# LayerNorm scale, shift and Strassen differences on row tiles, halves turned by DMA; low halves of q and of outputs ahead of p's, low products last

## The chip, the cores and the metric

The kernel runs on one core of one Trainium2 chip. The metric is the device time of one execution in microseconds (us). Before the change it is 1780.32 us, the median of three runs between 1778.46 and 1781.55 us. TensorE is called PE in the profile, VectorE DVE, ScalarE ACT, GpSimd POOL; SP is the queue that issues the DMAs.

## What is computed

One transformer block on 2048 rows of 512 values: LayerNorm with scale and shift from a condition vector, attention of 32 heads over the last 512 keys of a cache with 8 key heads, a gated residual, a second LayerNorm with scale and shift, a GEGLU network with 1792 hidden columns, a gated residual.

```
mod = (silu(c) @ w_mod).reshape(c.shape[0], 6, 1, -1)
sa, ca, ga, sb, cb, gb = mod[:, 0], mod[:, 1], mod[:, 2], mod[:, 3], mod[:, 4], mod[:, 5]
h = _layernorm(x) * (1 + ca) + sa
q = h @ wq;  s = q @ k.T * Dh ** -0.5;  p = softmax(s);  x = x + ga * ((p @ v) @ wo)
h = _layernorm(x) * (1 + cb) + sb
x = x + gb * ((gelu(h @ w_gate) * (h @ w_up)) @ w_down)
```

## The kernel before, in words

**Three products for one.** All operands are float32 values that are split in two float16 halves, a high one (ACT, rounding) and a low one (what is left, by DVE or POOL). `mm3` makes one product out of three float16 matmuls of 128x128 by 128x512 into one PSUM bank: low by high (line 86), high by low (line 87), high by high (line 88). The stationary operand comes first in the names, so in the scores the first of the three is the one that needs the low half of q.

**Stages.** The rows are treated in two halves of 1024. Four times, called gen 0 to 3, a normed half is prepared: gen 0 and gen 1 for the attention of half 0 and 1, gen 2 and gen 3 for the network of half 0 and 1. Each half consists of two blocks of 512 rows, and the products of a prepared half with the weights (q, and the network's first layer) are done by Strassen's scheme with seven instead of eight block products. It needs, transposed to columns on partitions and split in halves, the plain blocks b11, b21, b22 and the four differences t1 to t4.

**How gens 1 to 3 are prepared** (`ln_tile`, `combos`). A tile of 128 rows is loaded (in gen 2 it is the accumulator itself), DVE computes mean and variance, POOL the inverse root (line 386), DVE norms it in one instruction (line 466; ACT does it in gen 2, line 465), PE turns it by four float32 transposes into PSUM (line 471), ACT applies scale and shift by column in four instructions (line 479), the result `hf` is stored to DRAM (`hs`). In gens 1 and 2, ACT and POOL also make the halves of the plain blocks from it (lines 491, 493). When all eight tiles are done, `combos` loads the columns again (`cb`), POOL subtracts (line 510), ACT rounds (line 363), POOL makes the low half (line 367).

**The main loop.** Time in the attention runs in slots t = 0 to 511, one for each score tile of 128 rows by 512 keys. In slot t stand PE's scores of t; on DVE their maximum (line 914), the reciprocals of two row sums (line 931), the low half of p of slot t-3 (line 940), and then the things put into the slot's "d" list, among them the low halves of q and of the attention's outputs (line 676); on ACT the row sums' scaling (line 928), the exponential of t (line 923) and the high half of p of t-2 (line 935). Then SP issues a DMA transpose that turns p (line 944), and PE takes other products from a list. `run("d")`, `run("x")`, `run(t)` and `run("w")` are the places of a slot at which planned work is put in. Every engine works its list in order; SP too, so that a DMA which has to wait holds back those behind it. p is turned four slots at a time into `pt`, and the product with v (`po`) of unit u = t // 4 is taken two units later.

**Plans.** Loads into the five `raw` buffers are planned by `sched` (a position for the load's first use, from which the load goes ahead by up to three slots when the buffer's last user allows), others are put at a fixed slot by `at`, or between two slots by `within`. `mod_load` brings the weights from which DVE computes the scale and shift columns of the second LayerNorm (`wmc`, line 135), from slot 239 on.

Of the kernel before, what the change touches and what calls it, by code (L numbers as in the profile page):

```python
# [14 lines left out]
ALU = mybir.AluOpType  # L15
# [48 lines left out]
def block_kernel(ctx: ExitStack, tc: tile.TileContext, x, kT, v, wq, wo, wg, wu, wd, cT, wc, wm, out):  # L64
# [20 lines left out]
    def mm3(ps, lhi, llo, rhi, rlo, first, last, chain=False):  # L85
        nc.tensor.matmul(ps, llo, rhi, start=first, stop=False, skip_group_check=chain)  # L86
        nc.tensor.matmul(ps, lhi, rlo, start=False, stop=False, skip_group_check=chain)  # L87
        nc.tensor.matmul(ps, lhi, rhi, start=False, stop=last, skip_group_check=chain)  # L88
# [254 lines left out]
    NB = 14  # L343
    BK, hs, y1 = {}, {}, {}

    def spilled(gen, key):
        if (gen, key) not in hs:
            n = KT if key in (0, 1) else 2
            hs[gen, key] = dram.tile([P, n, QB], F32, name=f"hs{gen}_{key}")
        return hs[gen, key]  # L350

    def block(gen, name):
        if (gen, name) not in BK:
            BK[gen, name] = pool.tile([P, 4, QB], F16, tag="h", name=name, bufs=NB)
        return BK[gen, name]

    def stored(gen, name, p):
        qb, dt = {"b11": (0, p), "b21": (0, 2 + p), "y": (1, p), "b22": (1, 2 + p)}.get(name, (None, None))
        return spilled(gen, name)[:, p, :] if qb is None else spilled(gen, qb)[:, dt, :]

    def put(gen, name, p, src, eng):
        def high():
            nc.scalar.activation(block(gen, name)[:, p, :], src(), AF.Copy)

        def low():
            t = block(gen, name)
            eng.tensor_tensor(t[:, 2 + p, :], src(), t[:, p, :], op=ALU.subtract)

        return high, low

    def ln_cols(key):
        return (1, 0) if key == "a" else (4, 3)
# [40 lines left out]
    def ln_out(qb, dt):  # L413
# [11 lines left out]
        def affine(act=True):  # L425
            st["f"] = pool.tile([P, D], F32, tag="ot", name="hf", bufs=NOT) if qb else tmp("hf")
            if act:
                nc.scalar.activation(st["f"], st["ps"], AF.Identity, scale=cols[:, 1, dt:dt + 1], bias=cols[:, 0, dt:dt + 1])
            else:
                ts(st["f"], st["ps"], cols[:, 1, dt:dt + 1], cols[:, 0, dt:dt + 1], op1=ALU.add)  # L430
            dma(spilled(0, qb)[:, dt, :], st["f"])

        def direct():
            nc.scalar.activation(block(0, name)[:, p, :], st["ps"], AF.Identity, scale=cols[:, 1, dt:dt + 1], bias=cols[:, 0, dt:dt + 1])

        def low(eng=nc.vector):
            t = block(0, name)
            eng.tensor_tensor(t[:, 2 + p, :], st["f"], t[:, p, :], op=ALU.subtract)
# [5 lines left out]
    def ln_tile(gen, i, src):  # L444
        jsc, jsh = ln_cols("a" if gen < 2 else "f")
        qb, i = divmod(i % (2 * QT), QT)
        st = {}

        def load():
            if gen == 2:  # L450
                st["x"] = src()
            else:
                st["x"] = raw("xs")
                dma(st["x"], src())

        def stat():
            ln_stat(st["x"], st)
            ln_power(st)
            if gen == 2:
                st["nm"] = small.tile([P, 1], F32, name="nmean")  # L460
                pool_ts(st["nm"], st["mv"][:, 0:1], st["rs"], -1.0)

        def norm():
            if gen == 2:
                return nc.scalar.activation(st["x"], st["x"], AF.Identity, bias=st["nm"], scale=st["rs"])
            nc.vector.tensor_scalar(st["x"], st["x"], st["mv"][:, 0:1], st["rs"], op0=ALU.subtract, op1=ALU.mult)

        def turn():
            st["ps"] = bank("acc", "pln", NACC)
            for dt in range(KT):  # L470
                nc.tensor.transpose(st["ps"][:, dt * P:(dt + 1) * P], st["x"][:, dt * P:(dt + 1) * P], ident)

        def affine(dts):
            if 0 in dts:
                st["f"] = raw("hf") if gen == 2 else tmp("hf")
            f = st["f"]
            for dt in dts:
                sl = slice(dt * P, (dt + 1) * P)
                nc.scalar.activation(f[:, sl], st["ps"][:, sl], AF.Identity,
                                     scale=cols[:, jsc, dt:dt + 1], bias=cols[:, jsh, dt:dt + 1])  # L480
            if KT - 1 in dts:
                dma(spilled(gen, qb)[:, :, i * P:(i + 1) * P], f.rearrange("p (k q) -> p k q", k=KT))

        def parts(act):
            o = slice(i * P, (i + 1) * P)
            f = st["f"].rearrange("p (k q) -> p k q", k=KT)
            for h, name in enumerate(("b11", "b21") if qb == 0 else (None, "b22")):
                if name:
                    t, src = block(gen, name), f[:, 2 * h:2 * h + 2, :]
                    if act:  # L490
                        nc.scalar.activation(t[:, 0:2, o], src, AF.Copy)
                    else:
                        nc.gpsimd.tensor_tensor(t[:, 2:4, o], src, t[:, 0:2, o], op=ALU.subtract)

        more = [lambda: parts(True), lambda: parts(False)] if gen < 3 else []
        return load, [stat, norm, turn, lambda: affine((0, 1)), lambda: affine((2, 3))] + more

    def combos(gen, p, eng, base=True, d=0, e=0):
        X = {}

        def load(name):
            if gen == 0 and (p == 0 or name in ("b21", "b22")):
# [4 lines left out]
            dma(X[name], stored(gen, name, p))  # L507
# [4 lines left out]
        def parts(pos, name, tile_):  # L512
            high, low = put(gen, name, p, lambda: X[tile_], eng)
            return [(pos, high), (pos + 1 + e, low)]

        def plain(pos, name):
            return parts(pos, name, name) if base else []

        return [
            (lambda: load("b11"), plain(0, "b11") + [(2, diff("b11", "y", "b11"))] + parts(d + 4, "t1", "b11")),  # L520
            (lambda: load("y"), [(2, nop), (3, diff("y", "b22", "y"))] + parts(d + 5, "t3", "y")),
            (lambda: load("b22"), (plain(1, "b22") or [(2, nop)]) + [(4, diff("b22", "b22", "b11"))] + parts(d + 6, "t2", "b22")),
            (lambda: load("b21"), plain(3, "b21") + [(5, diff("b21", "b21", "b22"))] + parts(d + 7, "t4", "b21")),
# [262 lines left out]
    def product(key, gen, k, bank_of, start, stop):  # L786
        a, b = PROD[k]

        def group(p):
            c, off = COL[a]  # L790
            w, m = SET[key][c], BK[gen, b]
            sl = slice(off + p * P, off + (p + 1) * P)
            mm3(bank_of(), w[:, 0, sl], w[:, 1, sl], m[:, p, :], m[:, 2 + p, :], start and p == 0, stop and p == 1, True)
# [51 lines left out]
    def q_plain(u):  # L845
# [4 lines left out]
        def group(kt):  # L850
            if kt == 0:
                st["p"] = bank("acc", "pq", NACC)
            w, m, p = SET[u // 4][h % 2], BK[0, names[kt // 2]], kt % 2
            sl = slice(kt * P, (kt + 1) * P)
            mm3(st["p"], w[:, 0, sl], w[:, 1, sl], m[:, p, :], m[:, 2 + p, :], kt == 0, kt == KT - 1)
# [34 lines left out]
    def attn_final(ti):  # L890
# [3 lines left out]
        if ti < 2 * QT:  # L894
            own, steps = ln_tile(2, ti, lambda: acc[ti])
            own()
            for d, fn in zip((1, 4, 5, 6, 7, 9, 10), steps):
                at(("w", now[0] + d), fn)
            at(now[0] + 9, lambda: load_acc(nxt, rows_of(x, nxt)))
        else:  # L900
            at(now[0] + 3, lambda: load_acc(nxt, y1[nxt]))
# [15 lines left out]
    def expo(t):  # L917
# [6 lines left out]
        E[t].update(e=e, sm=sm)  # L924

    def recips(t):
        r = small.tile([P, 2], F32, name="rr", bufs=4)
        nc.scalar.activation(r, E[t]["sm"], AF.Copy, scale=1.0 / PSC)  # L928
        for k in range(2):
            E[t + k]["r"] = r[:, k:k + 1]  # L930
        return lambda: nc.vector.reciprocal(r, r)  # L931
# [55 lines left out]
    def q_first(warm):  # L987
        ps = bank("acc", "pq", NACC)
        for term, (a, b) in enumerate(((0, 0), (1, 0), (0, 2))):
            for kt in range(KT):  # L990
                w, m, p = SET[0][0], BK[0, ("b11", "b21")[kt // 2]], kt % 2
                nc.tensor.matmul(ps, w[:, a, kt * P:(kt + 1) * P], m[:, b + p, :], start=term + kt == 0, stop=term == 2 and kt == KT - 1)
# [4 lines left out]
    def begin():  # L997
# [10 lines left out]
        block(0, "y")  # L1008
        for name in ("b11", "b21", "b22", "t3", "t2", "t4", "t1"):
            block(0, name)  # L1010
# [94 lines left out]
    def sched_combos(gen, p, base):  # L1105
        for k, (load, steps) in enumerate(combos(gen, p, nc.gpsimd if gen or p == 0 else nc.vector, False, 0 if gen else 1 if p else 2, 0 if gen or p else 5)):
            if gen == 0 and (p == 0 or k > 1):
# [6 lines left out]
    for p in range(2):  # L1114
        sched_combos(0, p, CB[p])

    def plan_gen(gen, t_ln, t_cb, dcb, src):
        for i in range(2 * QT):
            t = t_ln[i]
            load, steps = ln_tile(gen, i, lambda i=i: src(i))  # L1120
            sched(t, (load, steps[:3]), t + 3, t + 5)
            for off, fn in zip((6, 7, 8, 9), steps[3:]):
                at(("w", t + off), fn)
        for p in range(2):
            sched_combos(gen, p, t_cb + dcb * p)

# [456 lines left out]
```

## Time and profile before

| | before |
|---|---|
| median of the runs | 1780.32 us (1778.46 to 1781.55) |
| span of the profiled execution, first to last instruction | 1775.9 us |
| its own time by the runs | 2.6 to 5.7 us of each run lie around such a span |
| PE / DVE / ACT / POOL busy | 98% / 81% / 68% / 49% |
| DMA engines, mean busy share | 0.80 over the span |
| chain that ended last, PE's share | 76% |

The profiled execution's own time is given as its span alone; the runs' times also hold what lies ahead of the first and behind the last instruction. A matmul of 512 columns is shown as 379 ns long, but the next one starts 216 ns after it, so that PE's busy share counts overlapped time, and a gap below some 160 ns between two matmuls does not show as idle time. Work is counted by the number of matmuls in a stretch instead.

### The profile page before, as it was taken

To read this page: it belongs to the slowest core of one execution; us is meant where nothing else is said; L and a number is where in the kernel's file an instruction comes from. 1 tells how busy PE (TensorE), PEld (TensorE's weight loads), DVE (VectorE), ACT (ScalarE), POOL (GpSimd) and SP (SyncE) were. 2 spreads that over 40 slices of the span, in tenths; PEclk is the share of its full clock that TensorE was granted. 3 is DMA by queue.
4 is the path that set the end of the run, shared out by engine and by line. 5 is a ranking of instruction groups with operands and counts; after the bars stand their busy time and mean duration, and the time that the engine had idled before them with its cause. 6 is when DMAs were issued, how large, how long until landed. Compare 5 with 4: busy or idle time off the path is not lost.

```text
span 1775.9 us, 25975 instructions
## 1 busy us (share of the span) xinstructions
PE 1732.4 (98%) x8112; PEld 796.0 (45%) x8114; DVE 1445.0 (81%) x2509; ACT 1216.4 (68%) x2822; POOL 877.5 (49%) x1103
## 2 busy tenths in 40 slices
PE   7899999999999989999999999999999999999999
PEld 4444444444444434444444444444444444444443
DVE  7888888888888889888888888888885768766676
ACT  5887787878878767887777777777774455434342
POOL 4879878776788873435565565555420024000000
PEclk9999999999999999999999999999999999999999
DMA  7999999999999997999999999999985543252222
GB/s 229 212 195 212 214 217 200 222 204 220 217 213 230 205 198 165 196 201 231 209 209 207 209 217 205 210 207 215 190 174 134 185 141 123 68 182 80 86 75 74
DMA packets 662122, 327.62 MB, mean 184 GB/s; under 512 B 553056, under 2 KB 575840, under 8 KB 661984
## 3 DMA queue, kind: packets, MB, share of 16 engines
q1 hardware_dynamic: 661696, 325.44, 79.8%
q8 instruction: 64, 1.05, 0.3%
q14 instruction: 74, 0.61, 0.1%
q10 hardware_dynamic: 288, 0.52, 0.1%
HBM read 131.73 MB, written 59.90 MB: 108 GB/s over the span
## 4 chain that ended last, share of the span: by engine, by line
PE 76%; DVE 12%; ACT 6%; issue 2%; DMA 2%; POOL 2%; SPq 0%; DVEq 0%; POOLq 0%; ACTq 0%
PE py L86 7%; PE py L87 7%; PE py L88 7%; PE ps L86 5%; PE ps L88 5%; PE ps L87 5%; PE po L86 4%; PE po L88 4%; PE po L87 4%; DVE p L940 3%; PE fa L86 3%; PE fa L88 2%; PE fa L87 2%; DVE nm L914 2%; PE qa L86 2%
## 5 line engine op out<-in xcount | busy, mean ns | idle before, releaser
L923 ACT ACTIVATE ee<-ps,nm 128x512 f32<-128x512 f32 x512 | 351.2, 686 | 256.4 <-DVE nm L914 250.6
L940 DVE SCALAR_TENSOR_TENSOR p<-ee,rr,p 128x512 f16<-128x512 f32 x512 | 467.1, 912 | 0.2
L914 DVE TENSOR_REDUCE nm<-ps 128x1 f32<-128x512 f32 x512 | 349.1, 682 | 83.5 <-PE ps L88 82.1
L935 ACT ACTIVATE p<-ee,rr 128x512 f16<-128x512 f32 x512 | 365.1, 713 | 0.9 <-DMA pt<-p 0.7
L86 PE MATMUL ps<-k,qt 128*128 128x512 f16 x512 | 194.3, 379 | 19.1 <-DVE qt L676 18.6
L86 PE MATMUL py<-wo,ot 128*128 128x512 f16 x512 | 194.1, 379 | 1.6 <-DVE ot L676 1.6
L88 PE MATMUL ps<-k,qt 128*128 128x512 f16 x512 | 194.2, 379 | 0.0
L87 PE MATMUL ps<-k,qt 128*128 128x512 f16 x512 | 194.2, 379 | 0.0
L87 PE MATMUL po<-pt,v 128*128 128x512 f16 x512 | 194.0, 379 | 0.0
L88 PE MATMUL po<-pt,v 128*128 128x512 f16 x512 | 194.0, 379 | 0.0
L87 PE MATMUL py<-wo,ot 128*128 128x512 f16 x512 | 194.0, 379 | 0.0
L88 PE MATMUL py<-wo,ot 128*128 128x512 f16 x512 | 194.0, 379 | 0.0
L86 PE MATMUL po<-pt,v 128*128 128x512 f16 x512 | 194.0, 379 | 0.0
L931 DVE RECIPROCAL rr<-rr 128x2 f32<-128x2 f32 x256 | 41.3, 161 | 95.8 <-ACT rr L928 94.4
L386 POOL TENSOR_TENSOR rs<-rs,nhalf 128x1 f32<-128x1 f32 x32 | 19.5, 609 | 187.3 <-DVE rs L380 99.1
L86 PEld LDWEIGHTS <-w 128*128 128x128 f16 x728 | 71.3, 98 | 88.7 <-DMA w<-kept 2.9
L87 PEld LDWEIGHTS <-w 128*128 128x128 f16 x728 | 71.3, 98 | 87.7 <-issue 3.2
L88 PEld LDWEIGHTS <-w 128*128 128x128 f16 x728 | 71.3, 98 | 86.3 <-issue 0.7
L884 DVE SCALAR_TENSOR_TENSOR acc<-py,dysc,acc 128x512 f32<-128x512 f32 x112 | 81.6, 746 | 28.8 <-PE py L88 28.0
L884 DVE SCALAR_TENSOR_TENSOR acc<-py,ysc,acc 128x512 f32<-128x512 f32 x128 | 94.6, 739 | 10.9 <-PE py L88 10.9
L923 ACT ACTIVATION_READ_ACCUMULATOR ee<-ps,nm 128x1 f32 x512 | 100.7, 197 | 0.0
L86 PEld LDWEIGHTS <-qt 128*128 128x128 f16 x512 | 50.3, 98 | 81.8 <-DVE qt L676 25.9
(267 smaller groups left out, 3859.6 us busy)
## 6 DMA issues: line engine op xcount, KB each, us to landing
w<-kept SPq DMA_DIRECT2D x123, 256.0 KB, 3.2
wo<-kept SPq DMA_DIRECT2D x60, 256.0 KB, 3.7
raw<-in_wo SPq DMA_DIRECT2D x56, 256.0 KB, 3.2
kept<-stage SPq DMA_DIRECT2D x56, 256.0 KB, 3.3
kept<-w SPq DMA_DIRECT2D x39, 256.0 KB, 3.4
rw<-in_wq SPq DMA_DIRECT2D x38, 256.0 KB, 3.3
hs<-hf SPq DMA_DIRECT2D x32, 256.0 KB, 2.7
pt<-p SPq DMA_TRANSPOSE x512, 3.5
```

Source lines behind the costliest of these rows:

```text
L86: nc.tensor.matmul(ps, llo, rhi, start=first, stop=False, skip_group_check=chain)
L87: nc.tensor.matmul(ps, lhi, rlo, start=False, stop=False, skip_group_check=chain)
L88: nc.tensor.matmul(ps, lhi, rhi, start=False, stop=last, skip_group_check=chain)
L386: nc.gpsimd.tensor_tensor(st["rs"], st["rs"], nhalf, op=ALU.pow)
L884: nc.vector.scalar_tensor_tensor(acc[ti], st["p"], by, acc[ti], op0=ALU.mult, op1=ALU.add)
L914: nc.vector.tensor_reduce(nm, E[t]["ps"], axis=AX.X, op=ALU.max, negate=True)
L923: nc.scalar.activation(e, E[t]["ps"], AF.Exp, bias=E[t]["nm"], scale=1.0, accum_out=sm[:, t % 2:t % 2 + 1])
L931: return lambda: nc.vector.reciprocal(r, r)
L935: nc.scalar.activation(p16[:, 0, :], E[t]["e"], AF.Copy, scale=E[t]["r"])
L940: nc.vector.scalar_tensor_tensor(p16[:, 1, :], E[t]["e"], E[t]["r"], p16[:, 0, :], op0=ALU.mult, op1=ALU.subtract)
```

## The change

Gens 1 to 3 are prepared in another way (`ln_pair`, with `plan_pair` for the slots). Two tiles, of the same place in the two blocks of 512 rows, go together. DVE applies mean, scale, inverse root and shift in two instructions on row tiles, with the scale and shift as rows that lie the same on all partitions (`ROWS`, stored and read back through DRAM). POOL makes the four differences on the row tiles, ACT the high and POOL the low halves into a tile that lies in the `raw` buffers, and SP turns both halves by one DMA transpose for each of B (b11 and b21), C (b22), T1 (t1 and t4) and T2 (t3 and t2). PE's transposes, ACT's scale and shift, the stores of `hf` and the loads of `cb` are gone from gens 1 to 3; gen 2 loads its tiles from the stored result of the attention. The blocks are laid out as the DMA transpose writes them, in gen 0 too. Gen 0 keeps its way otherwise.

```diff
     def mm3(ps, lhi, llo, rhi, rlo, first, last, chain=False):
-        nc.tensor.matmul(ps, llo, rhi, start=first, stop=False, skip_group_check=chain)
+        nc.tensor.matmul(ps, lhi, rhi, start=first, stop=False, skip_group_check=chain)
         nc.tensor.matmul(ps, lhi, rlo, start=False, stop=False, skip_group_check=chain)
-        nc.tensor.matmul(ps, lhi, rhi, start=False, stop=last, skip_group_check=chain)
+        nc.tensor.matmul(ps, llo, rhi, start=False, stop=last, skip_group_check=chain)
...
+    def row_store(j):
+        ROWS["d", j] = dram.tile([KT, P], F32, name=f"row{j}")
+        with nc.allow_non_contiguous_dma(reason="512 values"):
+            dma(ROWS["d", j].rearrange("k p -> p k"), cols[:, j, :])
+
+    def row_load(j):
+        ROWS[j] = pool.tile([P, D], F32, tag=f"row{j % 3}", name="row", bufs=1)
+        dma(ROWS[j], ROWS["d", j].rearrange("k p -> (k p)").partition_broadcast(P))
+
+    def ln_pair(gen, i, src):
+        by, shift = (1, 0) if gen < 2 else (4, 3)
+        X, S, st = {}, {}, [{}, {}]
...
+        def norm(k):
+            nc.vector.scalar_tensor_tensor(X[k], X[k], st[k]["mv"][:, 0:1], ROWS[by], op0=ALU.subtract, op1=ALU.mult)
+            nc.vector.scalar_tensor_tensor(X[k], X[k], st[k]["rs"], ROWS[shift], op0=ALU.mult, op1=ALU.add)
+
+        def sub(o, a, b):
+            def at_(n):
+                return X[n // 2][:, n % 2 * 256:n % 2 * 256 + 256]
+
+            nc.gpsimd.tensor_tensor(at_(o), at_(a), at_(b), op=ALU.subtract)
+
+        def alloc(s):
+            S[s] = pool.tile([P, 1 if s == 1 else 2, 2, 256], F16, tag="raw", name="turn", bufs=NRAW)
...
+        def high(s):
+            nc.scalar.activation(S[s][:, :, 0, :], side(s), AF.Copy)
+
+        def low(s):
+            nc.gpsimd.tensor_tensor(S[s][:, :, 1, :], side(s), S[s][:, :, 0, :], op=ALU.subtract)
+
+        def turn(s):
+            nc.sync.dma_start_transpose(block(gen, ("B", "C", "T1", "T2")[s])[:, i], S[s].rearrange("p a b c -> p (a b c)"))
...
     def attn_final(ti):
...
-        if ti < 2 * QT:
-            own, steps = ln_tile(2, ti, lambda: acc[ti])
-            own()
-            for d, fn in zip((1, 4, 5, 6, 7, 9, 10), steps):
-                at(("w", now[0] + d), fn)
-            at(now[0] + 9, lambda: load_acc(nxt, rows_of(x, nxt)))
-        else:
-            at(now[0] + 3, lambda: load_acc(nxt, y1[nxt]))
+        at(now[0] + 3, lambda: load_acc(nxt, rows_of(x, nxt) if ti < 2 * QT else y1[nxt]))
...
     def expo(t):
...
         E[t].update(e=e, sm=sm)
+        if t % 2:
+            r = small.tile([P, 2], F32, name="rr", bufs=4)
+            nc.scalar.activation(r, sm, AF.Copy, scale=1.0 / PSC)
...
     def recips(t):
-        r = small.tile([P, 2], F32, name="rr", bufs=4)
-        nc.scalar.activation(r, E[t]["sm"], AF.Copy, scale=1.0 / PSC)
...
+        nc.vector.reciprocal(E[t]["rr"], E[t]["rr"])
...
+    def plan_pair(gen, b, i, src):
+        load, stat, norm, sub, alloc, high, low, turn = ln_pair(gen, i, src)
+        for k in range(2):
+            within(b - 9 + k, b - 3 + k, lambda k=k: load(k))
+            at(("w", b + k), lambda k=k: stat(k))
+            at(("w", b + 3 + k), lambda k=k: norm(k))
+        for s, h, l, t in ((0, 6, 7, 8), (1, 7, 8, 9), (2, 10, 11, 12), (3, 11, 12, 13)):
+            sched(b + h, (lambda s=s: alloc(s), [lambda s=s: high(s), lambda s=s: low(s), nop]), b + l, b + t, ahead=0)
+            at(b + t, lambda s=s: turn(s))
+        at(("w", b + 8), lambda: sub(0, 2, 0), lambda: sub(2, 3, 2))
+        at(("w", b + 9), lambda: sub(3, 3, 0), lambda: sub(1, 1, 3))
+
+    for j in (0, 1):
+        at(60 + j, lambda j=j: row_store(j))
+        at(66 + j, lambda j=j: row_load(j))
...
+    for i in range(QT):
+        plan_pair(1, 78 + 32 * i, i, lambda k, i=i: rows_of(x, 2 * QT + QT * k + i))
+        plan_pair(2, 292 + 44 * i, i, lambda k, i=i: y1[QT * k + i])
...
             if t < T:
                 peak(t)
-            inv()
+            if t % 2 == 0 and 0 <= t - 2 < T:
+                recips(t - 2)
+            run(("d", t))
             if 0 <= t - LLAG < T:
                 low(t - LLAG)
-            run(("d", t))
...
-    nc = _bacc.Bacc("TRN2", target_bir_lowering=False, num_devices=1)
+    nc = _bacc.Bacc("TRN2", target_bir_lowering=False, num_devices=1, dynamic_dma_scratch_size=2048)
```

Gen 3 gets the same steps at places of the network's loop, and `combos` is left for gen 0 alone.

**DVE in an early unit.** The slot is number 22, which DVE works at 83 to 87 us of the trace. `nm` is the maximum of a score tile, `rr` the reciprocal of two row sums, `p` the low half of p, `qt` the low half of q, `w` that of a weight. Before:

```order
L914 TENSOR_REDUCE nm<-ps 128x1
L931 RECIPROCAL rr<-rr 128x2
L940 SCALAR_TENSOR_TENSOR p_1065<-ee,rr,p_1065 128x512
L676 SCALAR_TENSOR_TENSOR qt<-pq,qsc,qt 128x512
L676 SCALAR_TENSOR_TENSOR w_1079<-rw,wsc,w_1079 128x512
```

The same slot now:

```order
L905 TENSOR_REDUCE nm<-ps 128x1
L924 RECIPROCAL rr<-rr 128x2
L674 SCALAR_TENSOR_TENSOR qt<-pq,qsc,qt 128x512
L674 SCALAR_TENSOR_TENSOR w_1078<-rw,wsc,w_1078 128x512
L933 SCALAR_TENSOR_TENSOR p_1064<-ee,rr,p_1064 128x512
```

The low halves of q and of the weight moved ahead of p's.

**SP at the first pair of gen 1.** `pt` is a turned p, `hs` the stored columns, `B`, `C` and `T` the turned blocks, `turn` the tile with the two halves. Before, around the store of the first tile of gen 1:

```order
L944 DMA_TRANSPOSE pt<-p_3110 128x8x128
L94 DMA hs_0_3157<-hf 512x1x128
L944 DMA_TRANSPOSE pt<-p_3142 128x8x128
L94 DMA raw<-in_kT 128x512
L944 DMA_TRANSPOSE pt<-p_3175 128x8x128
L94 DMA raw<-in_wo 128x512
L944 DMA_TRANSPOSE pt<-p_3211 128x8x128
```

The same slots and the next ones now; p_3123 stands where p_3110 stood:

```order
L937 DMA_TRANSPOSE pt<-p_3156 128x8x128
L495 DMA_TRANSPOSE B<-turn 128x8x128
L94 DMA raw<-in_kT 128x512
L937 DMA_TRANSPOSE pt<-p_3186 128x8x128
L495 DMA_TRANSPOSE C<-turn 128x4x128
...
L495 DMA_TRANSPOSE T_3352<-turn 128x8x128
L94 DMA rw<-in_wq 128x512
L937 DMA_TRANSPOSE pt<-p_3338 128x8x128
L495 DMA_TRANSPOSE T_3390<-turn 128x8x128
L94 DMA kept<-x_3103 128x512
L937 DMA_TRANSPOSE pt<-p_3377 128x8x128
```

The four turns stand each right behind a transpose of p and ahead of the next one; each needs a low half by POOL.

**SP around slot 240.** `wmc` is a load for the scale and shift columns of the second LayerNorm, `cb` a load of `combos`. Before:

```order
L94 DMA wmc<-in_wc 128x512
L944 DMA_TRANSPOSE pt<-p_8188 128x8x128
L94 DMA cb<-hs_0_3157 128x512
L944 DMA_TRANSPOSE pt<-p_8218 128x8x128
...
L944 DMA_TRANSPOSE pt<-p_8337 128x8x128
L94 DMA wmc<-in_wc 128x512 x2
```

Now:

```order
L94 DMA wmc<-in_wc 128x512
L937 DMA_TRANSPOSE pt<-p_8022 128x8x128
L94 DMA kept<-x_7899 128x512
L937 DMA_TRANSPOSE pt<-p_8051 128x8x128
L94 DMA wmc<-in_wc 128x512
L937 DMA_TRANSPOSE pt<-p_8080 128x8x128
```

Before, the second of these loads stood six transposes of p behind the first, together with the third; now it stands two behind it.

More of the change, by code (lines that the diff above doesn't have):

```diff
@@ L436, in low @@
         def low(eng=nc.vector):
-            t = block(0, name)
-            eng.tensor_tensor(t[:, 2 + p, :], st["f"], t[:, p, :], op=ALU.subtract)
+            eng.tensor_tensor(part(0, name, 2 + p), by_rows(st["f"]), part(0, name, p), op=ALU.subtract)
         return turn, affine, low, direct
     xn = {}
[L444 to L451, printed above, removed]
-            else:
[L453 to L496, printed above, removed]
@@ L506, in load @@
                 X[name] = raw("cb")
[L507 removed]
+            dma(X[name], stored(name, p))
         def diff(o, a, b):
@@ L1103, in block_kernel @@
     at(256, lambda: mod_scale(3, "mf", 1.0, mx["m"]))
-    def sched_combos(gen, p, base):
-        for k, (load, steps) in enumerate(combos(gen, p, nc.gpsimd if gen or p == 0 else nc.vector, False, 0 if gen else 1 if p else 2, 0 if gen or p else 5)):
-            if gen == 0 and (p == 0 or k > 1):
+    for p in range(2):
+        for k, (load, steps) in enumerate(combos(p, nc.gpsimd if p == 0 else nc.vector, 1 if p else 2, 0 if p else 5)):
+            base = CB[p]
+            if p == 0 or k > 1:
                 at(base + ((0, 0, 0, 2)[k] if p else (-10, -2, -1, -9)[k]), load)
```

135 lines of the change are left out of this document (66 added, 69 removed).

## The prediction

> **What bounds the kernel now.** I read the page first, then the windows of 60 us, PE's waits, and the timeline at the longest of them.
>
> ```profile
> PE 1732.4 (98%) x8112; PEld 796.0 (45%) x8114; DVE 1445.0 (81%) x2509; ACT 1216.4 (68%) x2822; POOL 877.5 (49%) x1103
> ...
> 60.00:120.00 60.00, 50.96 (x239) 22.42 (x237) 52.27 (x91) 51.73 (x127) 44.36 (x52) 1.00 0.99 210
> 240.00:300.00 60.00, 60.00 (x285) 27.56 (x284) 52.05 (x94) 48.25 (x121) 48.84 (x64) 1.00 0.97 212
> 600.00:660.00 60.00, 55.07 (x250) 24.43 (x248) 49.40 (x84) 40.60 (x95) 49.74 (x57) 0.97 0.92 200
> 720.00:780.00 60.00, 55.84 (x265) 25.78 (x264) 50.04 (x96) 50.19 (x125) 24.78 (x35) 1.00 0.92 199
> 1140.00:1200.00 60.00, 60.00 (x283) 27.19 (x282) 52.01 (x89) 45.62 (x112) 29.56 (x40) 1.00 0.96 209
> 1500.00:1560.00 60.00, 60.00 (x279) 27.20 (x278) 43.04 (x67) 24.27 (x39) 0.00 (x0) 1.00 0.23 75
> ```
>
> The window rows give PE, PEld, DVE, ACT and POOL busy time with instructions, then PE's granted clock, the DMA share and GB/s. In the second, fifth and sixth stretch PE has no gap: 279 to 285 instructions in 60 us is all it does. There only fewer instructions on PE save time. In the first, third and fourth it does 239, 250 and 265, and who made it wait stands in its waits (total, times, longest):
>
> ```profile
> PE ps L86 <- DVE qt L676: 18.6, 12, 4.8
> PE pln L471 <- ACT acc L465: 5.6, 6, 2.4
> ...
> PE py L86 <- DVE ot L676: 1.6, 2, 0.9
> ```
>
> So PE sets the time, and the change can gain in two ways: instructions taken off PE, and these waits.
>
> **The change, part by part.** First PE's transposes.
>
> ```profile
> 239.36 0.38 PE L88 MATMUL po<-pt,v 128*128 128x512 f16 x1
> 239.58 0.60 PE L471 MATMUL pln<-ident,xs 128*128 128x128 f32 x4
> 240.01 0.38 PE L86 MATMUL ps<-k,qt 128*128 128x512 f16 x1
> ```
>
> From start to start a group of four takes 240.01 - 239.58 = 0.43 us. Gens 1 to 3 have 3 x 8 = 24 groups: 24 x 0.43 = **10.3 us** off PE, all on the path wherever PE has no gap. [...]
>
> The wait of the transposes for ACT's norm of `acc` in gen 2, **5.6 us**, goes with them; what is late next there is the turn on SP, which PE needs only at the network's start, 200 slots later.
>
> Now the waits for q. The typical one:
>
> ```profile
> 83.28 0.68 ACT L675 ACTIVATE qt<-pq,qsc 128x512 f16<-128x512 f32 x1
> 83.55 0.68 DVE L914 TENSOR_REDUCE nm<-ps 128x1 f32<-128x512 f32 x1
> 83.83 0.38 PE L88 MATMUL ps<-k,qt 128*128 128x512 f16 x1
> 84.69 0.17 DVE L931 RECIPROCAL rr<-rr 128x2 f32<-128x2 f32 x1 [0.46 <-ACT rr L928]
> 84.77 1.12 DVE L940 SCALAR_TENSOR_TENSOR p<-ee,rr,p 128x512 f16<-128x512 f32 x1
> 85.81 0.74 DVE L676 SCALAR_TENSOR_TENSOR qt<-pq,qsc,qt 128x512 f16<-128x512 f32 x1
> 86.61 0.39 PE L86 MATMUL ps<-k,qt 128*128 128x512 f16 x1 [2.40 <-DVE qt L676]
> ```
>
> q's high half is done at 83.96, its low half at 86.55, because DVE first waits for ACT's scaling of the row sums (now put right behind the exponential, a slot earlier) and then makes p's low half. In the new order the low half can follow the maximum and the reciprocal at 84.3 and end near 85.0. PE's first two matmuls need the high half alone and start at 84.05; the third, due 0.43 later, waits till 85.0: some 0.6 of the 2.57 us between the starts is left, 2.0 are saved, about 0.78. One of the twelve is another case:
>
> ```profile
> 646.49 1.13 SPq L94 DMA_DIRECT2D wmc<-in_wc  x2
> 649.72 0.84 DVE L135 SCALAR_TENSOR_TENSOR wmc<-wmc,sbc 128x512 f32<-128x512 f32 x1 [4.82 <-DMA wmc<-in_wc]
> 652.07 0.74 DVE L676 SCALAR_TENSOR_TENSOR qt<-qa,qsc,qt 128x512 f16<-128x512 f32 x1
> 652.86 0.61 PE L86 MATMUL ps<-k,qt 128*128 128x512 f16 x1 [4.83 <-DVE qt L676]
> ```
>
> DVE stood before a load that SP issued too late, since `combos` of gen 1 held the buffers. That load now stands four transposes of p earlier, so I count 4.0 of 4.8; the next late thing is DVE's own work. The eleven others are 18.6 - 4.8 = 13.8 us; 0.78 of it is **10.8 us**. If DVE were late for its own work alone, the order of the matmuls would still save 0.43 at each: 12 x 0.43 = 5.2 in place of 14.8. For the outputs' wait of 1.6 I count **1.0** by the same reasoning. Removed in all: 10.3 + 5.6 + 10.8 + 4.0 + 1.0 = **31.7 us**.
>
> What is added:
>
> ```profile
> L466 DVE TENSOR_SCALAR xs<-xs,mv,rs 128x512 f32<-128x512 f32 x16 | 8.7, 541 | 1.5 <-POOL rs L386 1.2
> L931 DVE RECIPROCAL rr<-rr 128x2 f32<-128x2 f32 x256 | 41.3, 161 | 95.8 <-ACT rr L928 94.4
> L884 DVE SCALAR_TENSOR_TENSOR acc<-py,ysc,acc 128x512 f32<-128x512 f32 x128 | 94.6, 739 | 10.9 <-PE py L88 10.9
> L479 ACT ACTIVATE hf<-pln,cols 128x128 f32<-128x128 f32 x96 | 37.8, 460 | 1.6 <-PE pln L471 1.6
> ```
>
> DVE norms 24 tiles by two instructions of about 0.74 (the row of L884 has such operands): 24 x 1.48 - 8.7 = 27 us more, against 94.4 us of waiting for ACT that goes; off the path. ACT loses L479's 37.8 and gets no more halves than before. Price on the path 0; if the cover were gone, DVE's 27.
>
> On SP the turns come between transposes of p, and each waits for POOL:
>
> ```profile
> pt<-p SPq DMA_TRANSPOSE x512, 3.5
> ...
> 245.13 3.47 POOL L730 TENSOR_TENSOR rw<-rw 128x256 f32<-128x256 f32 x4
> 251.05 1.74 POOL L493 TENSOR_TENSOR b<-hf,b 128x256 f16<-128x256 f32 x2
> 260.05 0.69 POOL L237 TENSOR_SCALAR gs<-gate,osc 128x512 f32<-128x512 f32 x1
> 263.99 1.23 SPq L944 DMA_TRANSPOSE pt<-p  x1
> 268.62 1.23 SPq L944 DMA_TRANSPOSE pt<-p  x1
> 276.97 0.38 PE L86 MATMUL po<-pt,v 128*128 128x512 f16 x1
> L157 POOL TENSOR_TENSOR w<-rw,w 128x512 f16<-128x512 f32 x50 | 66.5, 1330 | 4.2
> ```
>
> At gen 1's first pair POOL works from 248.6 to 260.7 what still stands ahead of the fourth half; 1.7 (L493) goes, four differences of 0.87 and four low halves (three of 1.33, one of about 0.8) come: 260.7 - 1.7 + 3.5 + 4.8 = 267.3. The fourth turn issues then, for 1.2 us, and the store behind it takes 0.6, so the transpose of p at 263.99 slips to about 269 and the unit's last one, with 0.6 and 1.2 us of issue for each of two steps, from 268.6 to about 272.5, 4 us. It landed 3.5 us after its issue and was read at 276.97, 8.35 after: 4.85 to spare. ACT's third high half needs the differences and holds the next exponential by some 2 us, which the second bank for scores covers. So the turns just fit. I take **4 us** of new waits over the eight pairs of gens 1 and 2, between 0 and 16 (2 us for each). The four small stores of rows and their loads I put at 0: a transfer lands in 3.5 us and one slot may slip that much.
>
> Sum against the profiled execution: 1775.9 - 31.7 + 4 = 1748.2 of span. The runs' median is 4.4 above the span, so **1752.6 us**.
>
> **The rivals.** *The turns hold up p (slower).* Place: SP in gens 1 and 2. If POOL's halves come 5 us later still (it is the busiest there, 48.84 of 60), p lands after its reader is ready, and PE idles 5 us for each pair. Such a gap costs more than itself: after the 4.83 us above the matmul took 0.61 in place of 0.38. With 1.5 us for that, 8 x 6.5 = 52 us: 1752.6 - 4 + 52 = **1800**. It decides from 31.7 / 8 = 4.0 us a pair. [...] For it: no turn has more than a slot between its half and its place on SP. Against: 4.85 us to spare in the case worked out, and POOL has but 29.56 of 60 in gen 2's stretch.
>
> *The DMA engines become the bound.*
>
> ```profile
> L944 SPq DMA_TRANSPOSE pt<-p x512: 1231/1232/2719, 37.8 to 1349.7; - x171
> ```
>
> Plain copies: 0.23 x 60 us for 75 GB/s x 60 us = 4.5 MB is 0.8 us for 256 KB. In the fifth stretch 57.6 us of DMA moved 12.5 MB, 23.4 transposes among it (512 in 1312 us); the other 6.4 MB are 19.7 us, so a transpose costs 1.6. Gens 1 and 2 get 24 full and 8 half turns, 45 us, and 8 loads, 6.4; 16 stores and 16 loads go, 25.6: 26 us more in 1000, on a share of 0.96. If that were already full, the time would be 1752.6 - 4 + 26 = **1775**. Against it: transposes land in 3.5 us with 8 to spare, and PE waits for no `pt`.
>
> *DVE is late for its own work.* Then the waits for q lose 5.2 alone, not 14.8: **1762**. *More goes*: all of the four waits and no new one, 10.3 + 5.6 + 18.6 + 1.6 = 36.1: **1744**, and a few us lower where the network's waits shrink too.
>
> **How the numbers follow.** Forecast 1753, 0.50 (its own range 1746 to 1760); DVE late 0.14; more goes 0.09; DMA bound 0.08; the turns hold up p 0.16; the gains eaten just up, no change, 0.03. A measurement of this kernel tells about 0.2% from no change, 3.6 us. Faster: 0.50 + 0.14 + 0.09 + 0.08 = 0.81; same 0.03; slower 0.16. The range reaches from 1742 to the DMA case with some margin, 1778, and leaves out the slower case and little else.
>
> **What would show it.** In the profile after: 96 fewer matmuls (8016), no `pln` after 40 us; PE's waits for `qt` near 4 us and in smaller pieces; no idle time of L931 for ACT; no DVE wait of 4.8 us for `wmc`; `po` waiting for DMA `pt` for at most a few us. I am wrong if `po` or `ps` waits tens of us at the turns (240 to 275, then every 82 us; in gen 2 from some 790 on), if pt's landing rises well above 3.5 us, or if the stretches of 60 us between 120 and 600 hold fewer matmuls than their transposes explain.

## The result: slower by 1.7%, and the profile after

The changed kernel takes 1810.54 us (median of four runs, 1809.63 to 1812.06), the kernel before 1780.26 us beside it (1778.46 to 1781.55). The ratio is 1.0172, 95% interval 1.0157 to 1.0186. The forecast was 1752.6 us, in a range of 1742 to 1778: wrong by 58 us, and in its sign.

The page of after gives the busy times; three rows of its windows of 60 us (PE, PEld, DVE, ACT and POOL busy with instructions, then PE's granted clock, the DMA share, GB/s) show where PE stood; then PE's longest waits (total, times, longest).

```profile
PE 1729.7 (96%) x8016; PEld 787.4 (44%) x8018; DVE 1458.1 (81%) x2541; ACT 1205.5 (67%) x2712; POOL 899.8 (50%) x1113
...
180.00:240.00 60.00, 44.58 (x200) 19.65 (x199) 36.61 (x65) 35.20 (x85) 36.53 (x44) 0.86 1.03 157
1020.00:1080.00 60.00, 48.78 (x208) 21.15 (x207) 41.62 (x76) 37.33 (x90) 27.94 (x39) 0.89 0.82 184
1140.00:1200.00 60.00, 52.85 (x239) 23.49 (x238) 48.42 (x86) 41.17 (x100) 38.03 (x47) 0.97 0.88 196
...
PE ps L86 <- ACT ee L914: 40.0, 26, 6.1
PE po L86 <- DMA kept<-x: 15.4, 1, 15.4
...
PE po L86 <- DMA pt<-p: 2.5, 4, 1.0
PE ps L88 <- DVE qt L674: 2.0, 2, 1.7
```

What was to go has gone: 96 matmuls (8112 to 8016), the waits for `qt` (18.6 to 2.0 us), the waits of the transposes for ACT. But three stretches that were nearly full have holes: 200, 208 and 239 instructions, where a full one has some 280. PE's clock is below 1 in them. One wait of 15.4 us is new, and PE's waits for the exponential are now 40.0 us in 26 pieces. The first two of these stretches before the change (the third, with 283, is in the prediction):

```profile
180.00:240.00 60.00, 59.90 (x284) 27.36 (x282) 52.67 (x96) 47.59 (x119) 44.35 (x58) 1.00 0.96 212
1020.00:1080.00 60.00, 60.00 (x282) 27.25 (x281) 50.42 (x87) 44.37 (x108) 38.00 (x49) 1.00 0.94 209
```

**The first hole** is the turn of p that arrives too late. The timeline of after, SP's queue (start, duration of the issue, what), and PE's first matmul behind the hole:

```profile
183.20 0.58 SPq L94 DMA_DIRECT2D row<-cols  x1
...
186.26 0.58 SPq L94 DMA_DIRECT2D row<-cols  x1
186.89 0.53 SPq L94 DMA_DIRECT2D kept<-x  x1
187.53 8.76 SPq L937 DMA_TRANSPOSE pt<-p  x1
196.33 0.58 SPq L94 DMA_DIRECT2D raw<-in_v  x1
197.02 4.08 SPq L937 DMA_TRANSPOSE pt<-p  x1
201.15 0.58 SPq L94 DMA_DIRECT2D kept<-w  x1
201.82 6.62 SPq L937 DMA_TRANSPOSE pt<-p  x1
...
208.53 0.59 PE L86 MATMUL po<-pt,v 128*128 128x512 f16 x1 [15.42 <-DMA kept<-x]
```

Behind the two stores of scale and shift columns (`row<-cols`) the issue of a transpose takes 8.76, 4.08 and 6.62 us in place of 1.23. The table of DMA issues of after has their landing (KB each, median us):

```profile
kept<-w SPq DMA_DIRECT2D x39, 256.0 KB, 3.0
...
row<-cols SPq DMA_DIRECT2D x4, 2.0 KB, 14.8
```

A store of 2 KB in 512 pieces of 4 bytes lands after 14.8 us in the median of four, one of 256 KB after 3.0. The two stores here take 19.2 us; the two of the second pair, at 708 and 710 us, take 10.4, and PE's two waits behind them are short, 1.0 and 2.3 us. The page puts PE's wait down to `kept<-x`, a store that stands right behind; PE does not read it, p's transposes stand behind it in the same queue.

**The second hole** is on ACT. The timeline of after, rows of ACT, SP and PE together:

```profile
1054.12 0.53 SPq L94 DMA_DIRECT2D raw<-in_wd  x1
1057.04 0.63 ACT L216 ACTIVATE junk<-raw 128x512 f16<-128x512 f32 x1 [6.21 <-DMA raw<-in_wd]
1058.48 0.59 PE L86 MATMUL ps<-k,qt 128*128 128x512 f16 x1 [5.11 <-ACT ee L914]
...
1067.66 1.23 SPq L495 DMA_TRANSPOSE T<-turn  x1
1070.78 0.63 ACT L489 ACTIVATE turn<-xs 128x512 f16<-128x512 f32 x1 [8.74 <-DMA T<-turn]
1072.12 0.59 PE L86 MATMUL ps<-k,qt 128*128 128x512 f16 x1 [6.11 <-ACT ee L914]
```

The halves to be turned lie in the five `raw` buffers. So the load of a weight came late, at 1054.12, and ACT, in order, stood 6.21 us before its norm with the next exponential behind. Then the fourth high half stood 8.74 us for the buffer that the third turn still held. PE's waits there were 5.11 and 6.11 us.

**The third hole** is on ACT too: at 1187.56 us it had stood 6.63 us before the third high half for a difference of POOL, and PE waited 4.9 us for the exponential behind it.

### The profile page after: what moved, and what is told of

Same layout as the page of the kernel before. It is cut to its first block, busy times and chain, and to the rows that moved or that the text cites. A ratio compares the mean times of both kernels' runs of the same rounds, so it can differ in the third digit from the quotient of the medians.

```text
span 1807.8 us, 25745 instructions
## 1 busy us (share of the span) xinstructions
PE 1729.7 (96%) x8016; PEld 787.4 (44%) x8018; DVE 1458.1 (81%) x2541; ACT 1205.5 (67%) x2712; POOL 899.8 (50%) x1113
## 4 chain that ended last, share of the span: by engine, by line
PE 76%; DVE 8%; DMA 5%; POOL 4%; ACT 3%; issue 3%; SPq 1%; POOLq 0%; DVEq 0%; ACTq 0%
PE py L86 7%; PE py L87 7%; PE py L88 7%; PE ps L86 5%; PE po L86 5%; PE po L87 5%; PE po L88 5%; PE ps L88 5%; PE ps L87 5%; PE fa L86 3%; PE fa L88 3%; PE fa L87 3%; DVE p L933 2%; PE qa L86 2%; PE qa L87 2%
## 5 line engine op out<-in xcount | busy, mean ns | idle before, releaser
L933 DVE SCALAR_TENSOR_TENSOR p<-ee,rr,p 128x512 f16<-128x512 f32 x512 | 453.1, 885 | 29.0 <-ACT p L928 28.8
L86 PE MATMUL po<-pt,v 128*128 128x512 f16 x512 | 195.0, 381 | 18.1 <-DMA kept<-x 15.4
L674 DVE SCALAR_TENSOR_TENSOR ot<-po,ot 128x512 f16<-128x512 f32 x128 | 87.1, 680 | 44.3 <-ACT ot L673 44.1
```

The source lines that it names most:

```text
L86: nc.tensor.matmul(ps, lhi, rhi, start=first, stop=False, skip_group_check=chain)
L674: return lambda: nc.vector.scalar_tensor_tensor(t[:, 1, :], src, scale, t[:, 0, :], op0=ALU.mult, op1=ALU.subtract)
L933: nc.vector.scalar_tensor_tensor(p16[:, 1, :], E[t]["e"], E[t]["r"], p16[:, 0, :], op0=ALU.mult, op1=ALU.subtract)
```

## The experiments

All ratios are against the kernel before on the same chip. A difference in us between two of the runs is one of their medians, and some of these come from different chips: the kernel before took 1779.6 to 1780.9 us beside them, so about 1 us of such a difference means nothing. The edits are shortened: helper lines and lambdas are left out.

**Rows without the small stores.**

```diff
-    at(60 + j, row_store(j)); at(66 + j, row_load(j))      # j = 0, 1; 3, 4 at 255, 262
+    def row_turn(j):                                       # at 60, 61, 258, 259
+        for dt in range(KT):
+            nc.tensor.transpose(ps[:, dt * P:(dt + 1) * P], cols[:, j, dt:dt + 1].to_broadcast([P, P]), ident)
+        nc.scalar.activation(ROWS[j], ps, AF.Copy)
```

> The changed kernel, but the four rows of scale and shift come from PE (four transposes each into a bank and one ACT copy) and not through four stores of 512 single values and four loads. If the small stores hold up the DMA queue, the gap of 15.6 us at 208 us goes, with it 1 to 2 us of low clock behind it; 16 transposes of 0.11 us come back, 1.7 us. Expected 1795 us (1791 to 1799), no po wait for DMA above 3 us. If the stall comes from something else (the kept stores alone, turns, a hiccup), it stays and the time is 1810 to 1814.

Measured 1790.6 us, ratio 1.0066 (1.0050 to 1.0083): 19.9 us less. The four loads that read the rows back, 256 KB each, are gone too; the next runs have the stores without them. The window of this kernel is full, and PE's waits of 1.0 and 2.3 us behind the second pair of stores are gone:

```profile
180.00:240.00 60.00, 60.00 (x287) 27.81 (x286) 53.44 (x99) 47.54 (x115) 45.27 (x60) 1.00 1.00 222
```

**The same stores in the kernel before**, which has none of the rest: two at slots 60 and 61, to a place that nobody reads; once as 512 pieces of 4 bytes, once as 128 of 16.

```diff
+    DUM[j] = dram.tile([KT, P], F32)                # second kernel: [P, KT]
+    dma(DUM[j].rearrange("k p -> p k"), cols[:, j, :])     # second kernel: dma(DUM[j], cols[:, j, :])
```

> The kernel before, with two stores added at slots 60 and 61, of 512 single values each to a DRAM tile that nobody reads. If these stores alone hold up the queue, whatever else the change does, PE stands some 15 us near 205 us and the time is 1780 + 15 to 17 = 1796 us (1793 to 1799). If the stall needs the other parts of the change (less time between p's turn and its reader, turns on the same queue), it is 1780 to 1785.

> The same two stores in the kernel before, of the same 2 KB each, but 128 pieces of 16 bytes in place of 512 of 4. If the price goes with the number of pieces, a quarter of 14.8 us to landing, some 4 us, fits into the time that p has to spare: 1780 to 1783 us. If it goes with the kind of store (any that is under some size), the stall is as long: 1794 to 1798.

Measured 1795.4 us, ratio 1.0077 (1.0059 to 1.0094), 14.5 us more, and 1781.1 us, ratio 0.9998 (0.9988 to 1.0007). Their tables of DMA issues, the first kernel and then the second:

```profile
row<-cols SPq DMA_DIRECT2D x2, 2.0 KB, 17.6
```

```profile
row<-cols SPq DMA_DIRECT2D x2, 2.0 KB, 2.2
```

The count of DMA packets below 512 bytes rises by 1056 in the first kernel and by 288 in the second. So two such stores alone do it, in an otherwise unchanged kernel. The same bytes in a quarter of the pieces land in an eighth of the time and cost nothing. Whether it is the number, the size or the places of the pieces that counts, the runs do not tell apart.

**The small stores on another queue**: issued by ACT.

> The changed kernel, with the four small stores issued by ACT on its own DMA queue in place of SP's. If the hold-up lies in the order of SP's queue, p's transposes pass the small stores and the gap near 208 us goes: 1794 us (1791 to 1798). If the engines that serve both queues, or the memory, are held up, it stays at 13 to 16 us: 1808 to 1813.

Measured 1811.2 us (one run), nothing gained, within the spread of the changed kernel. Issue table and window of this kernel:

```profile
row<-cols ACTq DMA_DIRECT2D x4, 2.0 KB, 14.0
...
180.00:240.00 60.00, 50.81 (x220) 22.00 (x219) 40.88 (x74) 37.32 (x91) 37.57 (x47) 0.91 1.08 171
```

The gap is split (4.3 us at 194, 4.9 at 204) and 6 us smaller; p still waits: ACT stands 6.38 us, up to 191.79, for a transpose of p that has not ended, and PE 7.0 us in five pieces for `pt` (2.5 in four in the changed kernel), though no such store stands in these transposes' queue. Behind the second pair of stores PE waits 3.3 and 2.6 us in place of 1.0 and 2.3. So the order of SP's queue alone is not the cause; by this run the hold-up lies in something that both queues share, and what that is was not shown.

**Turned tiles in buffers of their own.**

```diff
-    S[s] = pool.tile([P, 1 if s == 1 else 2, 2, 256], F16, tag="raw", name="turn", bufs=NRAW)
+    S[s] = pool.tile([P, 1 if s == 1 else 2, 2, 256], F16, tag="turn", name="turn", bufs=3)
-    sched(b + h, (alloc, [high, low, nop]), b + l, b + t, ahead=0)
+    at(("w", b + h), alloc, high); at(("w", b + l), low)
```

> The changed kernel, with the turned tiles in three buffers of their own in gens 1 and 2, not in those of the raw loads, and out of the planner's list for these. If the shared buffers make ACT stand before a load (6.21 us at 1057) and before a turn's DMA (8.74 us at 1070), the stretch from 1020 to 1080 loses 2 us of PE and not 16: expected 1796 us (1792 to 1801); the wait for POOL's differences at 1187 stays. If POOL's lateness itself is the cause, ACT waits for POOL in place of the DMA and the time is 1807 to 1811.

Measured 1792.2 us, ratio 1.0067 (1.0051 to 1.0083): 18.3 us less. The window of this kernel:

```profile
1020.00:1080.00 60.00, 56.65 (x265) 25.49 (x263) 49.92 (x92) 45.94 (x109) 35.87 (x47) 1.00 0.97 214
```

265 instructions for 208, the clock back at 1. PE's waits in it fall from 11.2 us to 3.3. The buffers were the cause there.

**Third and fourth halves a slot later.**

```diff
-    (2, 10, 11, 12), (3, 11, 12, 13)      # half, slot of high, low, turn
+    (2, 11, 12, 13), (3, 12, 13, 14)
```

> The changed kernel, with the third and fourth high half, low half and turn of each pair one slot later in gens 1 and 2. If ACT, in order, stands before POOL's differences, the 1.45 us at each of four pairs of gen 1 and some of the 5.1 us at 1189 go: expected 1801 us (1797 to 1805). If later turns only move the wait to SP and to the readers of p, or POOL slips with them, the time is 1808 to 1816.

Measured 1804.5 us, ratio 1.0142 (1.0125 to 1.0159): 6.0 us less, near the upper end of the range expected, and not where expected. PE's waits at gen 1's pairs, 1.29 us each (1.45 in the text above, which counts from start to start less the 0.22 of a matmul), were still there, 1.3 to 1.7; what went lay in gen 2 (241 instructions for 208 in the stretch from 1020 us, 248 for 239 in that from 1140). The larger part lies where ACT had stood before a shared buffer: its wait of 8.74 us became one of 3.5 and one of 1.4, for other things, while its wait for POOL's difference at 1187 us fell from 6.63 to 3.7 and PE's behind it from 4.9 to 2.8. So ACT's third high half was not what held PE in gen 1. The timeline of the changed kernel at the first pair shows what did:

```profile
253.43 0.74 DVE L933 SCALAR_TENSOR_TENSOR p<-ee,rr,p 128x512 f16<-128x512 f32 x1
254.09 1.10 DVE L472 SCALAR_TENSOR_TENSOR xs<-xs,mv,row 128x512 f32<-128x512 f32 x1
255.22 1.52 DVE L473 SCALAR_TENSOR_TENSOR xs<-xs,rs,row 128x512 f32<-128x512 f32 x1
256.67 0.68 DVE L905 TENSOR_REDUCE nm<-ps 128x1 f32<-128x512 f32 x1
257.38 0.69 ACT L914 ACTIVATE ee<-ps,nm 128x512 f32<-128x512 f32 x1 [3.33 <-DVE nm L905]
258.21 0.38 PE L86 MATMUL ps<-k,qt 128*128 128x512 f16 x1 [1.29 <-ACT ee L914]
```

DVE norms this row tile in 1.10 and 1.52 us, the maximum of the next scores stands behind it, ACT's exponential behind that, PE behind the exponential's bank.

**One norm instruction in a slot** follows from that reading.

```diff
-    at(("w", b + 3 + k), norm(k))                       # both instructions
+    for n in range(2):
+        at(("w", b + 3 + 2 * k + n), norm.parts[n](k))    # one each
```

> The changed kernel, with one instruction of DVE's norm in a slot and not two (scale in one slot, shift in the next, the second tile's behind them). If the gaps of 1.45 us at 258, 340, 422 and 504 us, and of 1.6 to 2.1 at 811 and 1170, come from two norm instructions of 1.1 and 1.5 us ahead of a maximum on DVE, they go: 6 to 9 us, expected 1803 us (1800 to 1806). If they come from ACT's third high half, which waits for POOL's differences, nothing goes: 1808 to 1813.

Measured 1807.0 us, ratio 1.0146 (1.0131 to 1.0161): 3.6 us less, between the two theories. At gen 1's pairs the wait of 1.29 us became one of 0.53, so DVE's norm was the cause there; a single norm instruction ahead of a maximum still leaves something. In gen 2 PE's wait of 1.44 us at 812 moved to another slot and grew: 2.20 us at 816, behind a norm instruction of 1.64.

**All four mends together, then two variants.** The first variant puts the third and fourth halves back; the second leaves them late in gen 2 alone and puts every turn one slot later on SP.

```diff
-    (2, 10, 11, 12), (3, 11, 12, 13)
+    (2, 11, 12, 13), (3, 12, 13, 14)                                     # all four
+    (0, 6, 7, 9), (1, 7, 8, 10), (2, 10, 11, 13), (3, 11, 12, 14)        # second variant, gen 1
+    (0, 6, 7, 9), (1, 7, 8, 10), (2, 11, 12, 14), (3, 12, 13, 15)        # second variant, gen 2
```

> The changed kernel with all four mends: rows by PE, turned tiles in buffers of their own, third and fourth halves a slot later, one norm instruction a slot. The runs so far gave 20, 18 and 6 us; the last two overlap in gen 2 (3 us left of the 6), and the norms are worth 6 to 9: 1810.5 - 20 - 18 - 3 - 7 = 1762 us (1757 to 1768), faster than before by 1%. If what goes in one place comes back in another, it stays above the 1766 us that the orders alone give to the kernel before.

> Three of the four mends (rows by PE, own buffers, one norm instruction a slot), the third and fourth halves back at their slots. In the run with all four, PE waits for p's DMA 2.3, 1.2, 2.3 and 1.3 us once a pair in gen 1, since the later turns stand ahead of p's transposes on SP. If that is what came back, these four waits go (8 us with their small ones), and gen 2 loses 3 us to POOL's differences again: 1771 us (1768 to 1774). If the own buffers cause it, because the loads that had waited for a shared buffer now crowd the queue, it stays at 1776 to 1780.

> As the run with three mends, but every turn's DMA is put one slot later on SP, and the third and fourth halves are later in gen 2 alone. If SP's waits for POOL's low halves, ahead of p's transposes, are what is left in gen 1, they go and gen 2 keeps its 3 us: 1766 us (1763 to 1770). If the later place of the turns only moves the collision with p, it is 1771 to 1778.

Measured 1776.6 us, ratio 0.9980 (0.9969 to 0.9991); 1775.8 us, ratio 0.9970 (0.9960 to 0.9979); 1769.9 us, ratio 0.9939 (0.9924 to 0.9954). The first two miss by 15 and 5 us, the third ends at the upper end of its range. PE's waits in the three, in this order, and the third one's busy times:

```profile
PE ps L86 <- ACT ee L929: 14.8, 21, 2.2
PE po L86 <- DMA pt<-p: 12.3, 11, 2.4
```

```profile
PE ps L86 <- ACT ee L929: 18.5, 27, 2.2
...
PE ps L88 <- DVE qt L689: 3.7, 2, 3.4
PE po L86 <- issue: 3.2, 1, 3.2
PE po L86 <- DMA pt<-p: 1.6, 3, 1.0
```

```profile
PE ps L86 <- ACT ee L929: 17.6, 26, 2.2
...
PE po L86 <- DMA pt<-p: 2.6, 5, 0.8
...
PE 1723.2 (98%) x8032; PEld 787.0 (45%) x8034; DVE 1462.1 (83%) x2541; ACT 1208.6 (68%) x2716; POOL 900.9 (51%) x1113
```

With the halves later, SP stands before turns that are not ready and p's transposes are late: 12.3 us, some 10 of it at the turns. Put back, these waits went, 1.6 are left; but in gen 2 and at the fourth pair other waits came (3.4 us at 528, 3.3 at 1053, 2.3 at 1157), so the time hardly moved. With the turns a slot later and gen 2's halves later too, these three shrink and 6 us go; SP's own waits for POOL's low halves fall from 4.0 to 1.7 us. The run changes both at once, so what each is worth stays open. What PE then still waits for is the exponential, 17.6 us in small pieces.

**The orders alone**, in the kernel before.

```diff
-    llo x rhi; lhi x rlo; lhi x rhi
+    lhi x rhi; lhi x rlo; llo x rhi
-    rr (ACT) ahead of the next exponential; low(p); run("d")
+    rr (ACT) behind the exponential; run("d"); low(p)
```

> The kernel before, with only the orders changed: the product with the low half of the moving side kept in the middle and that with the low half of the stationary side last, the scaling of the row sums behind the exponential, q's and the outputs' low halves ahead of p's. The prediction's terms for q and outputs give 10.8 + 1.0 = 12 us: 1768 us (1764 to 1772). If these waits were hidden behind others, the gain is under 4 us: 1776 to 1780.

Measured 1766.1 us, ratio 0.9924 (0.9910 to 0.9939): 14.1 us less, without any of the row tiles. One long wait was left, 4.7 us, for `wmc`.

**The orders, and `wmc` in two buffers of its own**, loaded three slots ahead.

```diff
-    t = raw("wmc")
+    t = pool.tile([P, 512], F32, tag="wmc", name="wmc", bufs=2)
-    sched(ts_[dt], (load, [step]))
+    at(ts_[dt] - 3, load); at(("w", ts_[dt]), step)
```

> The kernel before with the new orders, and the modulation's loads wmc in two buffers of their own, issued three slots ahead whatever the shared raw buffers hold. The wait of 4.88 us at 649 us goes if the shared buffers alone made that load late: 1766.1 - 5 = 1761 us (1759 to 1764). If DVE is late there for its own work or SP's queue is, 2 us or less go: 1764 to 1767.

Measured 1757.7 us (1757.3 to 1758.5), ratio 0.9879 (0.9862 to 0.9895): 8.4 us below the orders alone, more than the wait itself and below the range expected, and the fastest of all. The run also sets `dynamic_dma_scratch_size=2048`, as the changed kernel does and the run with the orders alone does not; what that does by itself was not tried. Its page and the first row of PE's waits:

```profile
PE 1728.4 (98%) x8112; PEld 796.7 (45%) x8114; DVE 1434.0 (82%) x2509; ACT 1243.1 (71%) x2822; POOL 890.2 (51%) x1103
...
PE ps L86 <- ACT ee L923: 6.5, 7, 2.0
```

It does 80 matmuls more than the best kernel with row tiles (8112 to 8032), and is 12.2 us faster.

## Why the prediction was wrong, step by step

**Right: the transposes, and the orders.** PE has 96 matmuls fewer; what they give by themselves no run shows. The waits for `qt` fell to 2.0 us (forecast near 4), `pt` lands after a median of 3.4 us (3.5 before), so the DMA engines did not become the bound, the waits for the norm of `acc` and for `wmc` are gone, and DVE's wait ahead of its reciprocals, 95.8 us before, is small (group of after: busy and mean ns, then idle time):

```profile
L924 DVE RECIPROCAL rr<-rr 128x2 f32<-128x2 f32 x256 | 39.0, 152 | 11.7 <-ACT rr L918 11.7
```

The orders were priced at 10.8 + 1.0 us; alone they gave 14.1. That the two are so close is in part luck: at the slots between 60 and 100 us PE still waits some 6 us, now for the exponential and no longer for `qt`, while the wait for the norm of `acc`, which was not counted there, fell from 5.6 to 2.0 us by the orders alone. The `wmc` wait, priced at 4.0 us, gave 8.4 once its load had buffers of its own; the clock behind the wait (0.94 in the stretch from 600 us with the orders alone, the first matmul 0.58 us long) is a part of that, as the prediction said of gaps. In that stretch PE does 279 instructions for 245, which is 34 x 0.216 = 7.3 us.

**The step that failed first: "the four small stores of rows and their loads I put at 0".** Without them the time fell by 19.9 us though PE's 16 transposes came in, and two of them alone cost 14.5 in the kernel before. The reason given was that a transfer lands in 3.5 us; that number was of p's transposes. Nothing in the trace showed a store in single values, so its cost was unknown; it should have had a range of its own, and not the value of another kind of transfer. In the changed kernel the two stores took 19.2 us to land, and PE stood 15.4.

**The second: the `raw` buffers.** The prediction worked out POOL's and SP's time at one pair of gen 1 and let it stand for all. It said nothing on who else needs the buffers in which the turned halves lie. In gen 2 weights for the network are prepared in the same five buffers: 18.3 us. It had even shown the like, the `wmc` load that came late since others held a buffer, and counted only that it would go.

**The third: "off the path" for DVE's norm.** The 27 us were priced by a row of 739 ns whose operand `py` comes from PSUM. In the norm both tensors lie in SBUF. The tile's rows in the changed kernel, gen 1's part and then gen 3's (min/median/max in ns):

```profile
L473 DVE SCALAR_TENSOR_TENSOR xs<-xs,rs,row x8: 752/1140/1526, 250.7 to 501.3; 128x512 f32<-128x512 f32 x8
```

```profile
L473 DVE SCALAR_TENSOR_TENSOR xs<-xs,rs,row x8: 731/744/746, 1433.6 to 1533.5; 128x512 f32<-128x512 f32 x8
```

Beside a busy POOL (227 of 270 us in gen 1's stretch from 240 us) it takes up to 1.53 us, in the network (POOL 39 of 120 us in gen 3's stretch from 1420) 0.74. The kernel before had a row that would have warned: p's low half (L940) has two operands in SBUF as well and takes 0.74 us in the median, up to 1.83 at most; one of 1.12 stands in the prediction's own lines. The row that gave the price (L884) stays at 726 to 752 ns in all its 240 instructions, at 732 to 744 between 300 and 600 us, where POOL is busy for 239 of the 300. The two in before (min/median/max in ns):

```profile
L940 DVE SCALAR_TENSOR_TENSOR p<-ee,rr,p x512: 722/743/1827, 36.9 to 1348.9; 128x512 f16<-128x512 f32 x171
```

```profile
L884 DVE SCALAR_TENSOR_TENSOR acc<-py,ysc,acc x128: 726/740/752, 110.6 to 1380.3; 128x512 f32<-128x512 f32 x128
L884 DVE SCALAR_TENSOR_TENSOR acc<-py,dysc,acc x112: 735/745/752, 1396.8 to 1772.1; 128x512 f32<-128x512 f32 x112
```

Why the rows with two operands in SBUF grow beside a busy POOL, these lengths do not tell. The average of DVE's idle time (94.4 us saved) said nothing on the slot: there the norm stands ahead of a maximum. Splitting it gave 3.6 us. The best kernel with row tiles has 17.6 us of waits for the exponential, the one without 6.5; by their neighbours some 6 of these 11 us more stand behind a norm instruction, and 3.1 (at 937 and 942 us) behind ACT's waits for loads of weights. That was read, not tried.

**SP's turns.** Of the 4 us little came: `po` waits 2.5 us for `pt` in the changed kernel, and 1.5 of them lie before the first turn, at 59, 88 and 99 us, where the kernel with the orders alone waits too. The slower rival, that the turns hold up p, was not what happened, so that its 1800 us lie near the measured time by chance; its mechanism is real, though, and appeared when the halves were moved a slot later (some 10 us). The 1.5 us a pair that it adds for what follows a gap was the author's estimate; the traces show this: before the change the seven matmuls behind the 4.83 us take 2.96 us from start to start (652.86 to 655.82), 1.45 more than 7 x 0.216, and in the changed kernel the eleven behind the 15.42 us take 4.56 (208.53 to 213.09), 2.2 more. ACT's third high half was covered in gen 1 as said, and not in gen 2, where POOL's difference came late at 1187 us: of the 6.0 us that the later halves gave, 2.1 of PE's waiting lie there.

**The account.** From before to after are 30.3 us. The orders bring -14.1. The small stores cost 19.9, the shared buffers 18.3, the order of the halves 6.0, the two norms in a slot 3.6, each as its own run against the changed kernel; these overlap, since three of them together give 34.8 and not 41.8. With every mend the row tiles stand at 1769.9 us, 3.8 above the orders alone and 12.2 above the orders with `wmc`. The 80 matmuls that they spare are 80 x 0.108 = 8.6 us by the transposes' own row (0.43 us from start to start for a group of four); against that PE is idle for 1766.3 - 1723.2 = 43.1 us of that profiled execution and for 1755.8 - 1728.4 = 27.4 of the one with the orders and `wmc`. More than the transposes gave went into waits, then; that these come from the work of DVE, POOL and SP in slots with little room is read from the rows above, and was not tried part by part.

## What to carry to other kernels

Price a DMA by its pieces, not by its bytes alone (2 KB landed after 17.6 us in 512 pieces and after 2.2 in 128), and look at what else has to move, on any queue, within the next 20 us: two stores of 2 KB held up a kernel that moves 327 MB. When work is moved into a shared buffer or onto an in-order engine, list who else needs the buffer in every stage, and what stands behind the instruction in its slot; an average of idle time does not tell. Test the parts of a change apart: here the small part (an order) was worth 14 us, the large one cost some 4 us even in the best of these runs.

## What the hardware did that was not expected

- 512 pieces of 4 bytes: 14.8 us to landing in the median (19.2 and 10.4 by pair), 17.6 in the kernel before; 128 pieces of 16 bytes: 2.2 us. While the first were under way, one transpose's issue on the same queue took 8.76 us in place of 1.23, and issuing the stores on another queue left the hold-up (1811.2 us against 1810.5).
- The norm's second DVE instruction, on two SBUF operands, 128x512 in float32, took 0.73 to 0.75 us in gen 3, where POOL was mostly idle (busy 39 of 120 us), and up to 1.53 in gen 1, where it was busy (227 of 270); in the kernel before, a row with an operand in PSUM took 0.726 to 0.752 throughout.
